# Earlier loads of the gate/up weights, and two corrected prices, in a planned transformer-block kernel

## The chip, the cores and the metric

The kernel runs on one core of a Trainium2 chip. That core has five engines with instruction queues of their own: TensorE (PE, matrix multiplications into the PSUM banks), VectorE (DVE), ScalarE (ACT), GpSimd (POOL) and SyncE (SP), which here only starts the transfers between memory and the on-chip buffer SBUF. The metric is device time in microseconds (us), the median of several runs. A measurement of this kernel can tell a change of about 0.2% (1.5 us) from none.

## The reference, cut to what matters

```python
xn = layernorm(x)                         # x: 2048 x 1024, bfloat16
q, k, v = split(xn @ wqkv)                # 32 heads of 32 columns
phi = lambda t: where(t > 0, t + 1, exp(t)) + 1e-6
pq, pk = phi(q), phi(k)
kv, z = einsum(pk, v), sum_over_rows(pk)  # per head
s = (pq @ kv) / (pq @ z + 1e-6) @ wo      # linear attention, 1024 columns
g = silu((silu(xn @ w_gate) * (xn @ w_up)) @ w_down)   # 3584 hidden columns
return x + s * g
```

## The kernel before, in words

All large products are computed with fast matrix multiplication of the Winograd-Strassen kind: seven half-size products take the place of eight, and the inputs and results of these are sums of blocks. For some of the seven products the scheme is applied a second time inside. So beside the matmuls there are many element-wise additions: of activations (`XF.outer`, `XF.inner`), of weights (`WF.combos` makes four sums of weight blocks, 1024 columns each; `WF.inner` makes up to eight smaller ones, of 256 and 512 columns) and of results (`Pair`).

The stages follow one another on TensorE: layer norm with the k and v projections (0 to about 120 us of the trace), the q projection (four "pairs", to about 195 us), gate and up (28 pairs over 14 groups of 256 columns, to about 520 us, with the softmax-free normalisation of q mixed in from the fourth pair to the eleventh), the attention output (four pairs, to about 575 us) and the down projection with the final gate (to the end). A pair is 1024 rows against 2 x 256 weight columns.

Nobody writes the order of the instructions by hand. Every operation is recorded in program order with what it reads and writes, and a planner (class `Plan`) then makes the order of each engine. It goes through all operations like a list scheduler with a price for each: at every step it takes the operation that can begin first, with ties broken by a due time `dl`. Each engine then runs its list strictly in order; semaphores hold it where a list item depends on another engine. The prices are only used to make the order. Three of the planner's rules matter here:

- **Weight loads.** `wload` records two transfers of 512 KB (gate and up, or the two halves of a q block), then `combos`. A load that is not marked `asap` gets, besides its true dependencies, a dependency on a TensorE step about 12 us ahead of its due time (`LEAD`, L316 and the loop over `o.sem` in `schedule`), so that it isn't started long before it is wanted. An `asap` load has none of that, and its due time is 6 us rather than 30 us behind the TensorE work recorded so far.
- **Where weights go.** There are three raw buffers (`raw_at`), three for the sums of four (`cmb_at`) and two for the inner sums (`inn_at`). Load number k takes raw buffer 0, 1, 0, 2, 1, 0, 2, ... The first two loads are the q blocks (Q0, Q1), then the groups G0 to G13 of gate and up, then four loads of normalised q for the attention output. Raw buffer 0 and raw buffer 2 are unused from the start; raw buffer 1 overlaps weights of the k and v stage.
- **The port.** VectorE and GpSimd share an SBUF port in the planner's view: an operation with `port = True` waits until GpSimd's current operation has ended, and GpSimd then waits for it. Marked are element-wise additions whose inputs both lie in SBUF, and line L1034.

GpSimd makes the inner sums of all gate/up weights (`IE`), and their sums of four except G0's (`CE`; G0's are VectorE's, `GC0`), 12 operations a group, and the inner sums of the attention output (`IS`). Everything else element-wise is on VectorE and ScalarE. All additions of `tt` are shown at line L478, all ScalarE operations at L470, all matmuls at L420.

`phi_evac` computes phi for a finished block: ScalarE's exponential, then L1034 (minimum and addition, fp16 in SBUF) and L1036 (maximum and addition), both on VectorE. L1036 reads the block from PSUM (`kind` "ps") or, where a last addition put the block into SBUF, from SBUF (`kind` "sb").

The names used below: "q pair (p, s)" is rows half p with q block s; "gate/up pair (p, n)" is rows half p with group n; x tiles are the 16 row tiles of the input; normalise operations are the additions' siblings at L478 that multiply phi(q) by 1/denominator.

Of the kernel before, what the change touches and what calls it, by code (L numbers as in the profile page):

```python
# [9 lines left out]
ALU = mybir.AluOpType  # L10
F32 = mybir.dt.float32
BF16 = mybir.dt.bfloat16
FP16 = mybir.dt.float16
KB = 1024
# [284 lines left out]
def build_kernel(nc, A_x, A_wqkv, A_wo, B_w_gate, B_w_up, B_w_down, out, WINDOW=20, NWARM=12, NIDLE=5, LEAD=12.0):  # L299
# [7 lines left out]
    NE = ("dve", "dve")  # L307
    CS, IS = ("dve",) * 4, ("pool",) * 8
    UBANK, PU = 0.0, 6.0
    N0, NA = 3, 2  # L310
    GC0 = ("dve",) * 4
    XE0 = XE1 = XE2 = XE3 = "dve"

# [8 lines left out]
    with ExitStack() as es:  # L322
# [61 lines left out]
        def tmp(pool):  # L384
            return VB(pool)

        def vap(v, dt=BF16, off=0, n=None):

            return SB.at(v.place + off, SIZE[v.pool.name] - off if n is None else n, dt)
# [4 lines left out]
        def sem(name):  # L394
            return es.enter_context(nc.semaphore(name))
# [4 lines left out]
        def dsem(name):  # L400
            if name not in semn:
                semn[name] = sem("d_" + name)
            return semn[name]
# [20 lines left out]
        def split(items):  # L424

            regs, vbs = [], []
            for x in items:
                if isinstance(x, VB):
                    regs.append(x.r)
                    vbs.append(x)  # L430
                else:
                    regs.append(x)
            return regs, vbs
# [22 lines left out]
        def op(eng, reads, writes, fn, busy, hold=(), **kw):  # L456
            rr, rv = split(reads)
            wr, wv = split(writes)

            mine = [v for v in rv if v.pool is BANK]  # L460
            wr += [v.r for v in mine if v not in wv]
            if mine:
                kw["urgent"] = kw.get("urgent", 0.0) + UBANK
            return PL.op(eng, rr, wr, fn, busy, vbs=rv + wv + list(hold), **kw)

        def ev(x):
            return x() if callable(x) else x

        def act(reads, writes, o, i, func, n, src="ps", **kw):
            return op("act", reads, writes, lambda h: h.activation(ev(o), ev(i), func, **kw),  # L470
                      n / 1200.0 + (0.055 if src == "ps" else 0.095) + (0.09 if "scale" in kw else 0.0)
                      + (0.09 if "bias" in kw else 0.0))

        def dve(reads, writes, fn, n, rate=0.96, **kw):
            return op("dve", reads, writes, fn, n / (rate * 1000.0) + 0.07, **kw)

        def tt(reads, writes, o, a, b, alu, n, fast=False, eng="dve"):
            f = lambda h: h.tensor_tensor(ev(o), ev(a), ev(b), alu)  # L478
            if eng == "pool":
                return op("pool", reads, writes, f, n / 610.0 + 0.42)  # L480
            q = dve(reads, writes, f, n, 1.92 if fast else 0.96)

            q.port = not any(isinstance(x, VB) and x.pool is BANK for x in reads)
            return q

        def dma(reads, writes, o, i, s, nbytes, tr=False, **kw):
            if tr:
                f = lambda h: h.dma_start_transpose(ev(o), ev(i))
            else:
                f = lambda h: h.dma_start(ev(o), ev(i))  # L490
            return op("sp", reads, writes, f, 1.25 if tr else 0.45, sem=s, nbytes=nbytes, **kw)
# [32 lines left out]
        class XF:  # L524
# [32 lines left out]
            def outer(self, parts):  # L557

                def g(nm):
                    return self.blk(nm) if parts == "all" else self.part(nm, parts)  # L560
                n = 2048 if parts == "all" else 512
                for o, a, b in (("T3", "R11", "R01"), ("T1", "R01", "R00"), ("T2", "R11", "T1"), ("T4", "R10", "T2")):
                    tt([g(a)[1], g(b)[1]], [g(o)[1]], g(o)[0], g(a)[0], g(b)[0], ALU.subtract, n, True)

            def inner(self, ms, eng="dve"):

                q = self.quad()
                bs = [JP.index(m) for m in ms]
                for u in range(0, len(bs), 2):
                    two = bs[u:u + 2]  # L570
                    lo, st = two[0], (two[1] - two[0] if len(two) > 1 else 1)

                    def cut(x):
                        return x[:, lo:two[-1] + 1:st]

                    def T(f):
                        o = self.j + f * 4 * KB
                        return cut(self.jform(f)[0]), both(*[SB.reg(o + b * KB, KB) for b in two])

                    def R(h, t):  # L580
                        return cut(q[:, :, h, :, t, :]), both(*[self.quarter_r(h, t, b) for b in two])
                    t2, t3, t4 = T(0), T(1), T(2)
                    for o, a, b in ((t3, R(1, 1), R(0, 1)), (R(0, 1), R(0, 1), R(0, 0)), (t2, R(1, 1), R(0, 1)),
                                    (t4, R(1, 0), t2)):
                        tt([a[1], b[1]], [o[1]], o[0], a[0], b[0], ALU.subtract, 512 * len(two), True, eng)
# [21 lines left out]
        class WF:  # L607
# [27 lines left out]
            def combos(self, eng):  # L635
                A = {(k, i): (self.v[:, :, 4 * k:4 * k + 4, i * 128:i * 128 + 128],
                              self.raw_r(None, range(4 * k, 4 * k + 4), i)) for k in range(2) for i in range(2)}
                C = [(self.c[:, q], self.cmb_r(q)) for q in range(4)]
                for n, (o, a, b, alu) in enumerate(((C[0], A[0, 1], A[1, 1], ALU.add), (C[1], C[0], A[0, 0], ALU.subtract),
                                                    (C[2], A[0, 0], A[0, 1], ALU.subtract),  # L640
                                                    (C[3], A[1, 0], C[1], ALU.subtract))):
                    tt([a[1], b[1]], [o[1]], o[0], a[0], b[0], alu, 1024, True, eng[n])
# [388 lines left out]
        def phi_evac(reads, src, kind, out_ap, out_r):  # L1031
            e = tmp(H1)
            act(reads, [e], partial(vap, e, FP16), src, ACT.Exp, 512, kind)
            dve([e], [e], lambda h: h.tensor_scalar(vap(e, FP16), vap(e, FP16), 1.0, EPS_PHI, ALU.min, ALU.add),  # L1034
                512, 3.84, urgent=PU).port = True
            dve(reads + [e], [out_r], lambda h: h.scalar_tensor_tensor(  # L1036
                out_ap, ev(src), 0.0, vap(e, FP16), ALU.max, ALU.add), 512, urgent=PU)

        kvb = [bank(leaves=False) for _ in range(3)]

# [189 lines left out]
        def wload(srcs, ceng, ieng, dt=BF16, reads=()):  # L1230
            k = wk[0]
            wk[0] += 1
            rk = (0, 1, 0)[k] if k < 3 else 2 - k % 3
            f = WF(raw_at[rk], cmb_at[k % 3], inn_at[k % 2], dt)
            for q, src in enumerate(srcs):
                if not isinstance(src, list):
                    src = [(slice(0, 8), src)]
                for kts, sr in src:
                    dma(list(reads), [f.raw_r(q, range(kts.start, kts.stop))], f.v[:, q, kts], sr,
                        dsem("wr%d_%d_%d" % (rk, q, kts.start)), 512 * KB // len(src))  # L1240
            f.combos(ceng)
            if ieng:
                f.inner(ieng, JQ)
            return f
# [3 lines left out]
        def q_load(s):  # L1248
            return wload([wqkv_v[:, :, (2 * s + q) * 256:(2 * s + q + 1) * 256] for q in range(2)], QC[s], QI[s])

        def gu_load(n):
            return wload([wg_v[:, :, n * 256:(n + 1) * 256], wu_v[:, :, n * 256:(n + 1) * 256]],
                         CE if n else GC0, None)
# [8 lines left out]
        def q_pair(p, s, wf, at=(), mix=()):  # L1262
            def evac(w, i, j, src, v, kind):
                g = 2 * (2 * s + w) + i
                o, orr = pq_tile(p, g, j)
                phi_evac([v], src, kind, o, orr)
            ST.pair(Pair(Prov(wf, XV[p]), evac, JQ), at, mix)
# [91 lines left out]
        def pq_load(p, j):  # L1359
            srcs = [[(slice(4 * k, 4 * k + 4), q_scr[p, k, j].rearrange("p (g t) -> p g t", t=512)[:, :, w * 256:(w + 1) * 256])  # L1360
                     for k in range(2)] for w in range(2)]
            return wload(srcs, CS, None, FP16, [named("q", p, k, j) for k in range(2)])
# [250 lines left out]
def bass_recurrent_scan__linear_attn_block__swiglu_ffn__prompt_kernel(  # L1613
    nc: bass.Bass,
    A_x: bass.AP,
    A_wqkv: bass.AP,
    A_wo: bass.AP,
    B_x: bass.AP,
    B_w_gate: bass.AP,
    B_w_up: bass.AP,  # L1620
    B_w_down: bass.AP,
    out: bass.AP,
):
    build_kernel(nc, A_x, A_wqkv, A_wo, B_w_gate, B_w_up, B_w_down, out)
# [28 lines left out]
```

## Time and profile before

| | |
|---|---|
| median of 16 runs | 761.14 us (756.64 to 763.69) |
| the profiled execution's own time | 760.1 us |
| its span, first to last instruction | 758.3 us |
| TensorE busy | 718.2 us (95%) |
| VectorE busy | 572.4 us (75%) |
| ScalarE busy | 358.7 us (47%) |
| GpSimd busy | 259.4 us (34%) |
| mean granted TensorE clock | 0.989 |

"Busy" counts the time in which an engine has an instruction in flight[...]. TensorE's busy time is all but the whole span, so what can be won without fewer matmuls is its idle time (about 40 us) and the time at a lowered clock.

By stage (TensorE busy, VectorE busy, GpSimd busy, of the stretch): 138 to 156 us: 17.73, 16.33 and 0.00 of 18; 164 to 195 us: 23.21, 29.59 and 23.82 of 31; 195 to 235 us: 37.40, 33.78 and 16.64 of 40; 235 to 335 us: 88.43, 87.51 and 64.76 of 100; 335 to 500 us: 165.00, 137.38 and 110.51 of 165.

### The profile page before, as it was taken

How to read it: one execution, taken by the hardware profiler on the slowest of the kernel's cores; microseconds unless marked ns; L12 is line 12 of the kernel's file. 1: busy time of each engine (PE TensorE's matmuls, PEld its weight loads, DVE VectorE, ACT ScalarE, POOL GpSimd, SP SyncE). 2: the span in 40 equal slices, each digit the busy share in tenths (PEclk: the TensorE clock that was granted, in tenths of full speed). 3: DMA queues.
4: the chain of work that ended last, by engine and by line, in shares of the span. 5: the costliest groups of instructions: out<-in, count | busy, mean ns of one | idle time of the engine just before them, and what ended most of it. 6: DMA issues, size and time to landing. Idle time of an engine off the chain costs nothing.

```text
span 758.3 us, 11444 instructions
## 1 busy us (share of the span) xinstructions
PE 718.2 (95%) x4091; PEld 388.5 (51%) x4121; DVE 572.4 (75%) x1107; ACT 358.7 (47%) x677; POOL 259.4 (34%) x230
## 2 busy tenths in 40 slices
PE   8999998896898988899999999999999999999996
PEld 4445454443455555556666666665554444444443
DVE  6999766989888789898888888879987662443433
ACT  3577554864546476564554554554565111111111
POOL 2111000029275478448765678802660000000000
PEclk9999999999999899999999999999999999999999
DMA  9343315250215536647333324145599382936421
GB/s 301 88 109 73 76 25 164 70 156 2 68 55 140 175 118 194 180 127 263 104 92 111 105 76 126 50 138 180 170 315 278 86 251 83 259 97 192 141 77 42
DMA packets 139801, 101.55 MB, mean 134 GB/s; under 512 B 18784, under 2 KB 132704, under 8 KB 139744
## 3 DMA queue, kind: packets, MB, share of 16 engines
q1 hardware_dynamic: 139744, 100.82, 44.6%
q8 instruction: 32, 0.52, 0.3%
q14 instruction: 25, 0.20, 0.1%
HBM read 68.16 MB, written 29.49 MB: 129 GB/s over the span
## 4 chain that ended last, share of the span: by engine, by line
PE 77%; DVE 16%; DMA 4%; issue 1%; ACT 1%; SPq 0%; ACTq 0%; DVEq 0%
PE ps L420 77%; DVE SB L478 8%; DVE ps L478 2%; DVE SB L1036 2%; DVE SB L1034 1%; DMA SB<-in_A_x_dram 1%; DMA SB<-h_scratch 1%; DMA SB<-in_B_w_up_dram 1%; ACT SB L470 1%; DMA SB<-m_scratch 1%; DVE stats L994 0%; DVE stats L995 0%; DVE SB L1286 0%; SPq L490 0%; DVE SB L1201 0%
## 5 line engine op out<-in xcount | busy, mean ns | idle before, releaser
L420 PE MATMUL ps<-SB 128*128 128x512 f16 (+3 forms) x3970 | 707.9, 338 | 31.3 <-DVE ps L478 10.6
L420 PEld LDWEIGHTS ps<-SB 128*128 128x128 f16 (+1 forms) x4000 | 382.6, 98 | 354.7 <-DVE ps L478 18.4
L478 POOL TENSOR_TENSOR SB<-SB 128x1024 f16<-128x1024 bf16 (+3 forms) x196 | 245.6, 1284 | 242.3 <-DMA SB<-in_B_w_up_dram 186.7
L470 ACT ACTIVATE SB<-ps 128x256 f32<-128x256 f32 (+4 forms) x397 | 214.4, 559 | 203.8 <-PE ps L420 190.7
L478 DVE TENSOR_TENSOR SB<-SB 128x512 f16<-128x512 f16 (+10 forms) x312 | 197.9, 667 | 71.7 <-DMA out_dram<-SB 21.6
L478 DVE TENSOR_TENSOR SB<-ps,SB 128x256 f32<-128x256 f32 (+2 forms) x318 | 182.7, 591 | 54.8 <-PE ps L420 49.9
L478 DVE TENSOR_TENSOR ps<-ps,SB 128x512 f32<-128x512 f32 (+1 forms) x238 | 122.3, 531 | 36.6 <-PE ps L420 31.4
L470 ACT ACTIVATE ps<-ps 128x512 f32<-128x512 f32 (+1 forms) x166 | 81.8, 494 | 120.8 <-PE ps L420 104.6
L470 ACT ACTIVATE SB<-SB 128x512 f16<-128x512 f32 x68 | 42.2, 620 | 57.8 <-DVE SB L478 57.2
L998 POOL TENSOR_TENSOR rstd<-veps,neg_half 128x1 f32<-128x1 f32 x16 | 11.2, 704 | 65.2 <-DVE veps L997 58.3
L1036 DVE SCALAR_TENSOR_TENSOR SB<-ps,SB 128x512 bf16<-128x512 f32 x49 | 32.9, 680 | 0.3
L1034 DVE TENSOR_SCALAR SB<-SB 128x512 f16<-128x512 f16 x64 | 23.3, 379 | 12.6 <-ACT SB L470 12.6
L470 ACT ACTIVATE SB<-SB,zc 128x512 bf16<-128x512 bf16 x32 | 22.1, 714 | 10.1 <-DVE SB L478 8.9
L470 ACT ACTIVATE SB<-SB,nmr,rstd 128x1024 f16<-128x1024 bf16 x12 | 14.8, 1234 | 1.1 <-DVE nmr L1000 1.0
L994 DVE BATCH_NORM_STATS2 stats<-SB 128x6 f32<-128x512 bf16 x16 | 11.0, 685 | 3.5 <-DMA SB<-in_A_x_dram 3.5
L1036 DVE SCALAR_TENSOR_TENSOR SB<-SB 128x512 bf16<-128x512 f32 x15 | 13.1, 876 | 0.1
L995 DVE BATCH_NORM_STATS2 stats<-SB 128x6 f32<-128x512 bf16 x16 | 10.9, 681 | 0.0
L420 PE MATMUL ps<-SB,ident 128*128 128x512 f16 x17 | 6.5, 558 | 1.4 <-POOL ident L501 1.4
L449 PE MATMUL ps<-ident,SB 128*128 128x128 f16 x40 | 3.0, 220 | 1.6 <-DVE SB L1201 1.0
L420 PEld LDWEIGHTS ps<-SB,ident 128*128 128x128 f16 x17 | 2.1, 131 | 4.5 <-issue 2.7
L1286 DVE RECIPROCAL SB<-SB 128x64 f32<-128x64 f32 x8 | 4.3, 539 | 0.0
L449 PEld LDWEIGHTS ps<-ident,SB 128*128 128x128 f16 x40 | 2.4, 98 | 3.5 <-DVE SB L1201 1.5
(28 smaller groups left out, 23.4 us busy)
## 6 DMA issues: line engine op xcount, KB each, us to landing
h_scratch<-SB SPq DMA_DIRECT2D x112, 128.0 KB, 1.7
SB<-h_scratch SPq DMA_DIRECT2D x16, 896.0 KB, 6.4
SB<-in_A_x_dram SPq DMA_DIRECT2D x32, 256.0 KB, 3.1
SB<-in_B_w_gate_dram SPq DMA_DIRECT2D x14, 512.0 KB, 4.1
SB<-in_B_w_up_dram SPq DMA_DIRECT2D x14, 512.0 KB, 5.3
SB<-in_B_w_down_dram SPq DMA_DIRECT2D x4, 1792.0 KB, 9.1
SB<-in_A_wqkv_dram SPq DMA_DIRECT2D x12, 512.0 KB, 6.8
SB<-r_scratch SPq DMA_DIRECT2D x32, 128.0 KB, 3.7
```

The lines of the kernel that those rows point to most:

```text
L420: last = h.matmul(o() if callable(o) else o, l() if callable(l) else l, r() if callable(r) else r, start=st, stop=sp, skip_group_check=True)
L449: last = h.transpose(o(), i(), ident[:, :])
L470: return op("act", reads, writes, lambda h: h.activation(ev(o), ev(i), func, **kw), n / 1200.0 + (0.055 if src == "ps" else 0.095) + (0.09 ...
L478: f = lambda h: h.tensor_tensor(ev(o), ev(a), ev(b), alu)
L994: dve([xr] + ([named("ve", 0)] if q == 1 else []), [sA], lambda h: h.bn_stats(stats[:, j, 0, :], xa[:, 0:512]), 512)
L995: dve([xr] + ([named("ve", 0)] if q == 1 else []), [sB], lambda h: h.bn_stats(stats[:, j, 1, :], xa[:, 512:1024]), 512)
L998: pool([ver, nh_r], [rsr], lambda h: h.tensor_tensor(rstd[:, j, :], veps[:, j, :], neg_half[:, :], ALU.pow), 0.56)
L1034: dve([e], [e], lambda h: h.tensor_scalar(vap(e, FP16), vap(e, FP16), 1.0, EPS_PHI, ALU.min, ALU.add), 512, 3.84, urgent=PU).port = True
L1036: dve(reads + [e], [out_r], lambda h: h.scalar_tensor_tensor(out_ap, ev(src), 0.0, vap(e, FP16), ALU.max, ALU.add), 512, urgent=PU)
L1286: dve([ea], [ra], lambda h, q=q: h.reciprocal(vap(ra, F32)[:, q * 64:q * 64 + 64], vap(ea, F32)[:, q * 64:q * 64 + 64]), 400)
```

## The change

Three edits, none of which changes what is computed or on which engine:

```diff
-    N0, NA = 3, 2
+    N0, NA, WA = 3, 2, True
...
             if eng == "pool":
-                return op("pool", reads, writes, f, n / 610.0 + 0.42)
+                return op("pool", reads, writes, f, n / 531.0 + 0.2)
...
             dve(reads + [e], [out_r], lambda h: h.scalar_tensor_tensor(
-                out_ap, ev(src), 0.0, vap(e, FP16), ALU.max, ALU.add), 512, urgent=PU)
+                out_ap, ev(src), 0.0, vap(e, FP16), ALU.max, ALU.add), 512, urgent=PU).port = kind == "sb"
...
                     dma(list(reads), [f.raw_r(q, range(kts.start, kts.stop))], f.v[:, q, kts], sr,
-                        dsem("wr%d_%d_%d" % (rk, q, kts.start)), 512 * KB // len(src))
+                        dsem("wr%d_%d_%d" % (rk, q, kts.start)), 512 * KB // len(src), asap=WA)
```

The first and the last make all of `wload`'s transfers `asap`: the q blocks, gate and up, and the loads for the attention output. The second changes the planner's price of a GpSimd addition: 2.10 to 2.13 us for 1024 columns, 1.26 to 1.16 us for 512, 0.84 to 0.68 us for 256. The third makes L1036 a port operation where it reads from SBUF.

Since the planner makes the order anew, every engine's list changes. The set of instructions is the same. The larger moves:

- SP's list. The two loads of Q0 and the two of G1, which stood after the last transposes and after the m_scratch stores, stand behind the transfers of x tiles 0 to 5 and of the k and v weights: Q0's two and G1's gate ahead of x tiles 6 and 7, G1's up ahead of x tiles 8 and 9. Each later gate and up load stands a few stores earlier, and the two are apart, each with its own wait on TensorE.
- GpSimd's list. G1's four sums of 1024 columns come before G0's inner sums instead of after them, and G1's inner sums are mixed with G0's. After that each group's four sums mostly stand together ahead of its inner sums.
- VectorE's and ScalarE's lists are reordered throughout, by a few places mostly; TensorE's list as well, within the planner's window of 20 steps.

## The prediction

> **What bounds the kernel now.** First the page's sums: TensorE is busy 718.2 of 758.3 us, so I looked for its gaps. The table of 20 us stretches puts them at the start, at 120 to 140 us and between 160 and 340 us; from 340 to 500 us TensorE has none, and nothing on another engine can be won there. TensorE's own timeline, reduced to rows with idle time in front (in brackets: us, and who ended it), has three large gaps:
>
> ```profile
> 181.20 4.46 PE L420 MATMUL ps<-SB 128*128 128x256 f16 x20 [4.82 <-DVE SB L1036]
> ...
> 247.60 32.30 PE L420 MATMUL ps<-SB 128*128 128x256 f16 x192 [3.62 <-DVE SB L478]
> ...
> 323.61 193.44 PE L420 MATMUL ps<-SB 128*128 128x256 f16 x1232 [3.31 <-DVE ps L478]
> ```
>
> All end on VectorE. The chain of waits names the work ahead of the first:
>
> ```profile
> 174.06 3.96 DVE SB L1034 x4
> 178.02 3.13 DVE SB L1036 x2
> ```
>
> Four L1034 take 3.96 us, whose median is 284 ns; 0.60 of the 3.13 us is an L1036 from PSUM, so the one from SBUF takes 2.5. The groups by shape show it for all:
>
> ```profile
> L1036 DVE SCALAR_TENSOR_TENSOR SB<-ps,SB 128x512 bf16<-128x512 f32 x49 | 32.9, 680 | 0.3
> L1034 DVE TENSOR_SCALAR SB<-SB 128x512 f16<-128x512 f16 x64 | 23.3, 379 | 12.6 <-ACT SB L470 12.6
> L1036 DVE SCALAR_TENSOR_TENSOR SB<-SB 128x512 bf16<-128x512 f32 x15 | 13.1, 876 | 0.1
> L478 POOL TENSOR_TENSOR SB<-SB 128x1024 f16<-128x1024 bf16 x39 | 84.6, 2184 | 105.6 <-DMA SB<-in_B_w_up_dram 105.4
> ```
>
> A stretched VectorE operation is about as long as a GpSimd sum of 1024 columns (2184 ns). The timeline at the second gap agrees, VectorE and then GpSimd:
>
> ```profile
> 240.40 5.48 DVE L478 TENSOR_TENSOR SB<-SB 128x512 f16<-128x512 bf16 x3
> 238.06 10.09 POOL L478 TENSOR_TENSOR SB<-SB 128x1024 f16<-128x1024 bf16 x7
> ```
>
> Last, busy time and granted clock (the 1.00 or less behind GpSimd's count) behind each gap:
>
> ```profile
> 181.00:185.00 4.00, 3.80 (x16) 2.17 (x17) 2.59 (x6) 1.95 (x4) 4.00 (x3) 0.57 0.00 0
> 246.00:253.00 7.00, 5.40 (x18) 2.64 (x19) 4.08 (x8) 1.57 (x4) 6.15 (x7) 0.51 0.17 56
> 324.00:328.00 4.00, 4.00 (x21) 2.35 (x19) 4.00 (x6) 3.19 (x7) 3.92 (x5) 0.58 0.13 49
> ```
>
> After each gap TensorE runs at half clock: that loses another 3.80 x 0.43 = 1.6, 5.40 x 0.49 = 2.7 and 4.00 x 0.42 = 1.7 us. So the three cost 6.4, 6.3 and 5.0 us, 5.9 on average: a third of all that can be won.
>
> [...] L1036 from SBUF stretches (to 2.6 us), L1036 from PSUM never does (at most 692 ns). [...] gaps of 3.3 to 4.8 us lead to half clock, the next largest after 20 us (1.93) doesn't. [...] Here x tiles issued at 3.83 us land 8.4 us later behind the weights.
>
> **The change, part by part.** Sums are against the profiled execution, 760.1 us (span 758.3); the runs' median is 1.04 higher.
>
> *Loads at the start.* Q0 and G1 move up, Q0 from 91 us and G1 from 165 us. Q0's pieces and G1's gate, 1.5 MB, lie ahead of x tiles 6 and 7 in SP's queue. [...] 1.5 MB at the measured 303 GB/s delay them by 5 us, from landing near 20 us (6 MB at that rate) to near 25; VectorE first reads them at 32.4. The up load (0.5 MB, 1.7 us) meets tiles 8 and 9 (issued 23.2, read at 38.8) and the first transposes (26.7, landing in 3.1, read at 32.1), which keep under 1 us. If that cover fails, VectorE, full from 12 to 37 us, stops: +2. I take +0.2. Q0's sums can't move: their buffers hold k and v data till about 120.
>
> *G1's sums.* Now GpSimd runs them at 175.5 to 184.6 us, across the first gap. Their buffer is last read by TensorE, one quarter after another, at 138, 146, 149 and 152 us by the trace's semaphore records, and the new list puts them there. GpSimd is empty then, and G0's inner sums behind them wait for weights until 161.2, so they delay nothing on GpSimd. What is left of GpSimd after 161 ends some 9 us earlier. Gains: the five stretched operations at 174 to 180 us take 6.5 us, unstretched 1.8; of the 4.7 between, 4.3 lie behind 175.5, on these sums. Short inner sums (0.7 to 1.2 us) take their place at about half a length for each of four, 1.8, so the gap shrinks by 2.5. It is then under 3.3, so the half clock goes: 1.6. Of the stretched ones at 186 to 190 (2.4 us) TensorE, idle 2.0 us at 185 to 193, gets 1.2. Cost: seven port operations lie at 149 to 155 us; two sums hold each up to 1.9 us, 3.8 together, against VectorE's 1.7 us of idle in the 18 from 138. TensorE is full there and has results in hand: I take 1.3. Sum: -4.0. If all waits moved rather than went: +1; if the whole first event goes free: -7.6.
>
> *G2 to G7.* The semaphore records give when the buffer is free: 184/190, 220/221, 242/243, 271/273, 298/299 and 327/329 us (gate/up), where the loads were issued at 200, 227, 256, 280, 308 and 336. So GpSimd begins each group 6 to 16 us earlier. Its work isn't awaited by TensorE (no such row in the waits), so this is worth nothing by itself; what counts is where the sums of 1024 fall. G3's, landing 5.7 us after 221, end near 235.5, so the three operations at 240.4 meet short inner sums: their 5.48 us become about 3.3, the gap 1.4: -2.2, and -2.7 for the clock. G6's end near 313.5, so the gap at 320.3 shrinks by 1.4 and loses its half clock: -3.1. Against this, G5's would begin near 278, just where six normalise operations lie (277 to 283), and in the new list two of them stand ahead of G4's last sum and two right behind G3's. I count one new event of the average size, +5.9. Sum: -2.1.
>
> *G8 on.* 7 to 8 us earlier, TensorE full: 0. *Attention output.* Its first load comes 14 to 31 us earlier, out of the way of the m_scratch loads; TensorE idles 1.8 us at 500 to 545: -0.6 (-1.5 to +1).
>
> *SP's queue.* Gate and up wait for TensorE separately, with h stores queued behind them. Freeing comes 1.3 to 1.5 us apart (for G2 6), so a store waits about that long; h buffers are twelve. 0; a store chain that emptied them would stop ScalarE.
>
> *L1036's mark* affects 15 operations, with (876 - 680) x 15 = 2.9 us of waiting in all, part of the sums above. *GpSimd's prices*: new 2.13/1.16/0.68, measured 2.18/1.21/0.74 to 0.86, so the group of twelve is priced 15.9 rather than 16.8, its measured length 15.5 to 17.0: no clear correction. Only through the order: 0, within the range.
>
> Sum: 0.2 - 4.0 - 2.1 - 0.6 = -6.5, so 753.6 for this execution, 754.6 for the median.
>
> **Rivals.** Let n be the number of new events, a pair of port operations under sums of 1024; each is 5.9 and the rest of the sum is -12.4. For an event speaks that 40 additions with both inputs in SBUF lie at 160 to 335 us and that the planner's times are not the chip's; against it that the planner now starts loads from buffers TensorE frees, and knows L1036's wait.
> - None: 748.7. Needs the new order to fit the chip's times everywhere.
> - Two: 760.5, no change. GpSimd's work has only been moved against VectorE's.
> - Slower: three or more, in the normalise stage, where GpSimd is busy 65% and VectorE 88%. 5.3 x 1 over, so 766.4 for three. It decides from n = 2.1 on. The before has three events in all; the new order would need as many among the groups G2 to G7 and G1's new place.
> - The early loads don't help since their transfers are paced by the buffers anyway: true from 340 us on, and it would leave the first gap, about 760.
>
> **How the numbers follow.** Likeliest, n = 1: 0.38, own range 751 to 758. None: 0.15. Two, or mere moving: 0.21, of which 0.09 faster, 0.08 same, 0.04 slower, since about 0.2% (1.5 us) is what can be told from none. Three or more: 0.26, of which 0.02 same. Faster 0.38 + 0.15 + 0.09 = 0.62, same 0.10, slower 0.28. The range leaves out half of n = 0 and those beyond three: 748 to 766.
>
> **What would show it.** Right: GpSimd's 1024 sums at 138 to 154 us; the 4.82 us gap under 3 and no half clock near 181; GpSimd's wait for up weights (186.7 us) much smaller; L1036 from SBUF at a mean near 700 ns. Wrong: new half-clock stretches between 195 and 335 us, normalise operations over 1 us behind sums of 1024, or VectorE waiting for x tiles before 40 us.

## The result, and the profile after

The changed kernel takes 748.24 us (median of 9 runs, 746.22 to 750.75), the kernel before 760.94 beside it (median of 48 runs). The ratio is 0.983, with a 95% interval of 0.9811 to 0.9849: faster by 12.7 us, about twice the 6.5 us that the prediction summed up. The profiled execution took 747.62 us, its span is 745.9, TensorE is busy 713.7 us of it and the mean clock is 0.995. Of the 12.4 us by which the span shrank, 4.5 are TensorE's busy time (between 130 and 560 us it runs at half clock for 3.4 us, in the kernel before for 13.7) and 7.9 its idle time.

TensorE's timeline between 130 and 340 us, changed kernel, rows with over 1.5 us of idle time in front (start, length, what ran, in brackets the idle time and who ended it):

```profile
136.18 0.81 PE L420 MATMUL ps<-SB 128*128 128x256 f16 x4 [1.58 <-ACT ps L470]
...
176.89 8.44 PE L420 MATMUL ps<-SB 128*128 128x512 f16 x46 [1.72 <-DVE SB L478]
...
258.57 27.95 PE L420 MATMUL ps<-SB 128*128 128x256 f16 x174 [2.37 <-DVE SB L478]
```

The three gaps of 4.82, 3.62 and 3.31 us are gone, and so is the one of 1.93 us at 281.8. The chain of waits ahead of 177 us still has the same four L1034:

```profile
172.98 3.25 DVE SB L1034 x4
176.24 0.60 DVE SB L478
177.17 1.19 DVE SB L1036 x2
```

The groups by shape (busy us, mean ns; then idle before) and the wait of GpSimd for the up weights (us in all, times, longest) are:

```profile
L1036 DVE SCALAR_TENSOR_TENSOR SB<-ps,SB 128x512 bf16<-128x512 f32 x49 | 32.4, 678 | 0.1
L1034 DVE TENSOR_SCALAR SB<-SB 128x512 f16<-128x512 f16 x64 | 23.8, 388 | 12.1 <-ACT SB L470 12.1
L1036 DVE SCALAR_TENSOR_TENSOR SB<-SB 128x512 bf16<-128x512 f32 x15 | 12.5, 843 | 0.0
```

```profile
POOL SB L478 <- DMA SB<-in_B_w_up_dram: 89.0, 13, 8.1
```

GpSimd waits for up weights 89.0 us rather than 186.7, so the loads do come early. But the operations that GpSimd's sums hold are hardly shorter: L1036 from SBUF 843 ns against 876, L1034 388 against 379. To see all of VectorE's waiting at once, I took from each trace, for every kind and shape of VectorE operation, the time by which an instance exceeds the lower quartile of its kind: 43.5 us before, 44.4 after. The waiting has not gone. It lies elsewhere: of the operations held for over 1 us between 195 and 335 us there were six before (begun at 217, 240, 243, 291, 318 and 321 us) and two after (253 and 255).

Where the time went shows in the busy times by stretch. Columns: stretch, its length; busy time (and instructions) of TensorE's matmuls, its weight loads, VectorE, ScalarE, GpSimd; granted clock; share and GB/s of the transfers. The kernel before:

```profile
0.00:138.00 138.00, 129.30 (x714) 63.07 (x728) 112.40 (x275) 81.32 (x136) 13.86 (x34) 1.00 0.42 116
138.00:164.00 26.00, 25.27 (x167) 13.55 (x168) 22.49 (x56) 19.93 (x42) 1.17 (x1) 1.00 0.39 118
164.00:195.00 31.00, 23.21 (x115) 10.96 (x114) 29.59 (x48) 16.28 (x30) 23.82 (x19) 0.94 0.14 36
195.00:235.00 40.00, 37.40 (x262) 22.17 (x261) 33.78 (x68) 18.89 (x40) 16.64 (x12) 1.00 0.38 107
235.00:335.00 100.00, 88.43 (x535) 53.17 (x534) 87.51 (x153) 61.14 (x118) 64.76 (x48) 0.95 0.47 143
335.00:500.00 165.00, 165.00 (x1066) 103.70 (x1064) 137.38 (x248) 84.90 (x174) 110.51 (x84) 1.00 0.38 116
500.00:570.00 70.00, 68.09 (x412) 39.39 (x411) 62.77 (x104) 38.17 (x79) 28.66 (x32) 1.00 0.71 221
```

The changed kernel:

```profile
0.00:138.00 138.00, 127.06 (x701) 61.22 (x714) 109.78 (x270) 79.75 (x132) 14.11 (x34) 1.00 0.46 123
138.00:164.00 26.00, 22.68 (x116) 11.30 (x116) 25.37 (x51) 19.54 (x39) 8.82 (x4) 0.93 0.29 91
164.00:195.00 31.00, 28.20 (x181) 14.34 (x180) 29.87 (x57) 18.43 (x36) 15.31 (x16) 1.00 0.20 59
195.00:235.00 40.00, 38.50 (x273) 23.52 (x272) 36.57 (x73) 21.49 (x44) 28.51 (x20) 1.00 0.27 82
235.00:335.00 100.00, 94.55 (x601) 57.52 (x599) 91.41 (x168) 64.11 (x126) 65.36 (x49) 1.00 0.56 180
335.00:500.00 165.00, 163.77 (x1048) 101.78 (x1047) 136.31 (x247) 83.21 (x170) 101.27 (x79) 1.00 0.35 110
500.00:570.00 70.00, 69.91 (x413) 39.99 (x412) 61.26 (x101) 41.91 (x84) 28.74 (x31) 1.00 0.77 237
```

With the idle time as stretch less busy time, and the loss at a low clock estimated as stretch times what is missing to 1.00, the change comes to:

| stretch, us | idle | clock | sum |
|---|---|---|---|
| 0 to 138 | +2.2 | 0 | +2.2 |
| 138 to 164 | +2.6 | +1.8 | +4.4 |
| 164 to 195 | -5.0 | -1.9 | -6.9 |
| 195 to 335 | -7.2 | -5.0 | -12.2 |
| 335 to 500 | +1.2 | 0 | +1.2 |
| 500 to 570 | -1.8 | 0 | -1.8 |

The sum is -13.1, 0.7 more than the span shows, since the stretches hold slightly different work. Nearly all of the gain lies in the stage where normalisation and gate/up overlap, 195 to 335 us.

### The profile page after: what moved, and what is told of

The parts are those of the page before. It is cut to its first block, busy times and chain, and to the rows that moved or that the text cites. A ratio compares the mean times of both kernels' runs of the same rounds, so it can differ in the third digit from the quotient of the medians.

```text
span 745.9 us, 11430 instructions
## 1 busy us (share of the span) xinstructions
PE 713.7 (96%) x4092; PEld 386.4 (52%) x4121; DVE 568.5 (76%) x1107; ACT 358.4 (48%) x677; POOL 262.1 (35%) x230
## 4 chain that ended last, share of the span: by engine, by line
PE 75%; DVE 18%; issue 2%; DMA 2%; ACT 2%; SPq 0%; ACTq 0%; DVEq 0%
PE ps L420 75%; DVE SB L478 9%; DVE SB L1036 3%; DVE ps L478 2%; DVE SB L1034 2%; ACT SB L470 1%; DMA SB<-in_A_x_dram 1%; DMA SB<-SB 1%; DVE stats L994 1%; DVE stats L995 1%; ACT ps L470 0%; DVE SB L1286 0%; DVE Zh L1205 0%; SPq L490 0%; DVE SB L1201 0%
## 5 line engine op out<-in xcount | busy, mean ns | idle before, releaser
L470 ACT ACTIVATE SB<-SB 128x512 f16<-128x512 f32 (+1 forms) x68 | 42.2, 621 | 77.5 <-DVE SB L478 74.7
L1034 DVE TENSOR_SCALAR SB<-SB 128x512 f16<-128x512 f16 x64 | 23.8, 388 | 12.1 <-ACT SB L470 12.1
L1036 DVE SCALAR_TENSOR_TENSOR SB<-ps,SB 128x512 bf16<-128x512 f32 x49 | 32.4, 678 | 0.1
L1036 DVE SCALAR_TENSOR_TENSOR SB<-SB 128x512 bf16<-128x512 f32 x15 | 12.5, 843 | 0.0
```

The source lines that it names most:

```text
L1036: dve(reads + [e], [out_r], lambda h: h.scalar_tensor_tensor(out_ap, ev(src), 0.0, vap(e, FP16), ALU.max, ALU.add), 512, urgent=PU).port = ...
```

## The experiments

Four theories were set against each other, and the expectations name them so. A: early loads let GpSimd's long sums (1024 columns) run clear of VectorE's port operations. B: better prices give a better order. C: any new order is a draw, and that of before was a poor one. D: it is the order of VectorE's work and the times of GpSimd's sums that must fit each other, so early loads without the new order, or the new order without early loads, gain nothing. "Held" says that a VectorE operation takes longer than it does without a GpSimd sum beside it: the trace shows it as one long instruction, an L1036 from SBUF of 2.60 us beside long sums and of 0.79 with these cut. "The port" is the planner's name for what holds it; which part of the chip that is, no run shows. All ratios are against the kernel before on the same chip, with 95% intervals.

### The edits one by one

The loads alone (first and last edit of the diff), the mark on L1036 alone, the new price alone, and then the loads with one of the other two. Mark and price together without the loads were not tried.

```diff
# loads alone
+    N0, NA, WA = 3, 2, True
+                        dsem(...), 512 * KB // len(src), asap=WA)
# mark alone
+                out_ap, ev(src), 0.0, vap(e, FP16), ALU.max, ALU.add), 512, urgent=PU).port = kind == "sb"
# price alone
+                return op("pool", reads, writes, f, n / 531.0 + 0.2)
```

> The earlier loads alone, without the two price corrections. Theory A (the loads move GpSimd's sums of 1024 columns away from VectorE's port operations, and that is the gain): most of the 1.7%, 748 to 752 us, no half-clock stretch between 160 and 335 us. Theory B (the gain is the better order that the planner makes once it knows L1036's wait and GpSimd's times): 758 to 762 us. Theory C (any new order lands somewhere between 748 and 766 by chance, and the parts don't add up): anything, and the sum of the parts alone is not the whole.

> The port mark of L1036 from SBUF alone. Theory A: 759 to 762 us, since only 2.9 us of waiting in all is at stake. Theory B: 752 to 757 us. Theory C: anything within 748 to 766.

> GpSimd's new price alone. Theory A: 759 to 763 us, no change, since the new price of a group of twelve is no nearer to the measured one than the old. Theory B: 752 to 758 us. Theory C: anything within 748 to 766.

> Earlier loads and the port mark, with GpSimd's old price. Theory A: 747 to 751 us, the whole gain. Theory B: about 752 to 757, as the port mark alone. Theory C: not the sum of the two parts alone.

> Early loads and the new price of GpSimd's additions, without the mark on L1036; it completes the set of one, two and three edits. If the edits' effects add (loads -1.14%, price -0.74%), ratio 0.981, as the whole change, and the mark is worth nothing. If the mark is what makes the loads fit (loads with mark gave 0.987, loads alone 0.989), about 0.988 and half clocks after 200 us. If each order is a matter of chance, anything between 0.980 and 1.0.

| kernel | median us | ratio | 95% interval |
|---|---|---|---|
| loads | 752.04 | 0.9886 | 0.9829 to 0.9943 |
| mark | 761.40 | 1.0018 | 1.0001 to 1.0035 |
| price | 754.50 | 0.9926 | 0.9905 to 0.9947 |
| loads + mark | 750.33 | 0.9868 | 0.9812 to 0.9924 |
| loads + price | 753.91 | 0.9901 | 0.9880 to 0.9921 |
| all three | 748.24 | 0.9830 | 0.9811 to 0.9849 |

The effects don't add: the price is worth 0.7% alone, where theory B had it, and on top of the loads it costs 0.15%. Nor do the loads alone do what theory A asked: the time is at the edge of its range, but half clock comes in at 183 and 204 us (granted clock 0.97 from 138 to 195 us, 0.91 from 195 to 235). What holds is the mean: the four kernels with early loads have a mean ratio of 0.987, the three without (the kernel before among them) 0.998. The mark's three comparisons give +0.2, -0.2 and -0.7%, the price's -0.7, +0.2 and -0.4%. So the loads carry about 1.1%; the other two can't be told from the scatter of orders, which the last experiment measures.

### Is it the port?

If the port is what it is about, the gain must vanish once GpSimd's sums are short. In two kernels each weight sum on GpSimd is cut to the first 8 columns of its last dimension, a sixteenth of its columns in all, in the kernel before and in the changed one; in a third only the sums of 1024 columns, in the kernel before. The rest of these sums is left out of the computation. The order of all lists and the prices stay as they were.

```diff
-                return op("pool", reads, writes, f, n / 610.0 + 0.42)
+                return op("pool", reads, writes, lambda h: h.tensor_tensor(cut(ev(o)), cut(ev(a)), cut(ev(b)), alu), n / 610.0 + 0.42)
...
+def cut(x):
+    return x[(slice(None),) * (len(x.shape) - 1) + (slice(0, 8),)]
```

> The kernel before with each of GpSimd's weight sums cut to 8 columns of its last dimension (the rest of the sums is left out), the order unchanged: GpSimd holds the port for a small part of the time. What it gains is the whole price of the port waits. Theory A and D: three gaps, three half clocks and the smaller waits go, 738 to 746 us. If the port is not the cause: 757 to 762 us.

> The changed kernel with GpSimd's weight sums cut in the same way (the rest left out). Theory A and D: what the change gained was port waits, so with these gone in both the two short kernels lie within 4 us of each other: 738 to 746 us. If the gain came from the order apart from the port: it is kept, some 10 us below the short kernel before.

> The kernel before with its order unchanged; only GpSimd's additions of 1024 columns are cut to 8 columns, so that part of the sums of four weight blocks is left out; the inner sums are whole. With all of GpSimd's weight sums cut the time was 734.6, 26.6 us less. The prediction let only the long sums cost anything: about 735 to 738 by it. If the cost goes by GpSimd's busy time (52 long sums at 2.18 us are 113 of 259 us), 26.6 x 0.44 = 12, so about 749.

The kernel before with short sums takes 734.62 us (ratio 0.9657, 0.9618 to 0.9695), the changed one 731.93 (0.9629, 0.9593 to 0.9665), both below the forecast, and with only the long sums cut the kernel before takes 741.80 (0.9747, 0.9725 to 0.9770). So GpSimd's sums cost the kernel before 26.6 us and the changed one 748.24 - 731.93 = 16.3. With sums this short (the waiting counted as above is 6.0 and 5.7 us), the two orders are 2.7 us apart instead of 12.7: some 10 us of the gain come from where GpSimd's sums fall. That TensorE waited for the sums themselves is ruled out: in the traces of both kernels there is no such wait. The long sums alone cost 761.56 - 741.80 = 19.8 us, three quarters of it, though they are 112.4 of the 250.6 us of these sums. The small ones are not free: about 7.

VectorE's timeline shows this at one place. The third kernel has the list of before, so the operations are the same. First the kernel before, then the one with its long sums cut:

```profile
173.99 4.04 DVE L1034 TENSOR_SCALAR SB<-SB 128x512 f16<-128x512 f16 x4
177.95 2.60 DVE L1036 SCALAR_TENSOR_TENSOR SB<-SB 128x512 bf16<-128x512 f32 x1
```

```profile
175.23 2.23 DVE L1034 TENSOR_SCALAR SB<-SB 128x512 f16<-128x512 f16 x4
177.38 0.79 DVE L1036 SCALAR_TENSOR_TENSOR SB<-SB 128x512 bf16<-128x512 f32 x1
```

The same five operations take 6.6 us beside the long sums and 3.0 beside small and cut ones; TensorE's gap there falls from 4.82 to 1.50 us. Left out work also ends earlier, so the 26.6 and 19.8 us are upper bounds on what the held operations cost.

### Early loads without the new order, and the new order without early loads

One kernel keeps every compute list of before and only moves the weight loads in SP's list to right behind what frees their buffer. The other has all lists of the changed kernel, but the loads of G2 to G13 get back the TensorE step that held them. Both helpers act after planning and touch SP's list alone: `early` takes the `LEAD` step from each weight load and moves the load up, `held` gives it back and moves the load down.

```diff
# lists of before, loads early (on the kernel before)
-                        dsem(...), 512 * KB // len(src))
+                        dsem(...), 512 * KB // len(src)).wl = True
-        prog = PL.emit(esem)
+        early(PL); prog = PL.emit(esem)
# lists of the change, loads late (on the changed kernel)
-        prog = PL.emit(esem)
+        held(PL); prog = PL.emit(esem)
```

> The lists of TensorE, VectorE, ScalarE and GpSimd are those of the kernel before, word for word, and their buffers too; only the weight transfers start as soon as their buffer is free (Q0's and G1's behind the first fourteen transfers). GpSimd then begins G2 to G13 some 6 to 14 us earlier, while G1's sums stay behind G0's inner sums. Theory A in its plain form (earlier sums by themselves miss VectorE's port operations at 240 and 320 us): those two gaps and their half clocks go, 8 us, and new collisions near 280 us give some back: 751 to 757 us. Theory D (the new order of VectorE's list is what misses the sums, and the earlier loads only let the planner make it): 759 to 766 us, collisions elsewhere.

> The lists of the changed kernel, but the loads of G2 to G13 are held back by the TensorE step of the old rule, so that GpSimd begins each group 6 to 14 us later than the order was made for. Theory A: the collisions come back, 755 to 762 us. Theory D: they come back as well, perhaps more (756 to 766), since the order fits the early sums. If neither the sums' place nor the port matters: 748 to 750 us.

Early loads with the old order: 777.32 us, ratio 1.0216 (1.0181 to 1.0252), 16 us slower than before. The new order with late loads: 765.44, 1.0063 (1.0044 to 1.0083), 17 us slower than the changed kernel and 5 slower than before. TensorE's timeline of the first (rows of over 3.5 us of idle time):

```profile
181.40 4.46 PE L420 MATMUL ps<-SB 128*128 128x256 f16 x20 [5.13 <-DVE SB L1036]
...
203.02 0.61 PE L420 MATMUL ps<-SB 128*128 128x256 f16 x2 [3.87 <-DVE SB L478]
...
263.99 7.76 PE L420 MATMUL ps<-SB 128*128 128x512 f16 x38 [5.20 <-DVE ps L478]
...
297.67 15.01 PE L420 MATMUL ps<-SB 128*128 128x512 f16 x86 [8.39 <-DVE ps L478]
```

And what lies ahead of the largest, on VectorE and on GpSimd in the same kernel:

```profile
286.62 10.38 DVE L478 TENSOR_TENSOR SB<-SB 128x512 f16<-128x512 bf16 x7
```

```profile
287.28 9.44 POOL L478 TENSOR_TENSOR SB<-SB 128x1024 f16<-128x1024 bf16 x4 [6.89 <-DMA SB<-in_B_w_up_dram]
```

Four of these seven operations take 2.33 us each, a long sum's length, where the kernel before took 0.41. There they were over at 281.2 us and this group's sums began at 286.1; with early loads the sums begin while the operations run. The other three gaps have such holds ahead of them as well. This refutes A as it stood: earlier loads by themselves move the long sums onto port operations as readily as off them, and the loss is 11 us beyond what D forecast. With the old order, early loads don't gain.

The kernel with the new order and late loads doesn't show the other half of D. Its largest gap, 5.35 us, ends at 238.48, with four long sums running from 233.40. But the chain of waits ahead of it leads elsewhere:

```profile
228.89 5.73 DMA SB<-r_scratch
...
236.02 2.42 DVE SB L478 x2
```

The first row is a load of the denominators for the normalisation. In SP's list it stands right behind the weight loads that are held back: it is issued at 228.89 us and lands 5.73 us later, where the changed kernel issues it at 225.17 and has it 2.84 us later. One of the two normalise operations behind it is held, 2.07 us for 0.41. The gaps that end at 267.05 and 297.63 go back to such loads too, and ScalarE waits 13.3 us for them between 195 and 335 us, in the changed kernel not at all. So this kernel loses at least in part by SP's queue, and what the new order is worth without early loads stays open.

One number of the first kernel matters for the prediction: at the end of the k and v stage (131 us) it is only 0.1 us behind the kernel before, measured at the same TensorE step, although Q0's and G1's loads stand between the x tiles (G1's gate is issued at 17.2 us, its up at 20.0). Their transfers cost all but nothing.

### Q0 and G1 late

```diff
-                        dsem(...), 512 * KB // len(src), asap=WA)
+                        dsem(...), 512 * KB // len(src), asap=WA and k not in (0, 3))
```

> The changed kernel, but the loads of Q0 and of G1 are not marked: they stand where the kernel before had them, and G1's sums follow G0's inner sums again. The loads of Q1, G0 and G2 onwards are early. The prediction's terms for these two loads were +0.2 at the start and -4.0 for G1's sums: by them this kernel is 3.8 us slower than the changed one, about 752. By the progress measured since (start +2.3 us, q projection about -2.2 us net) the two cancel: 748, with the first gap and its half clock back near 181 us and the start 1 to 2 us quicker. If the order after 200 us is a matter of chance, since every list is planned anew, it is anything from 748 to 760, with half clocks between 235 and 335 us.

757.79 us, ratio 0.9945 (0.9931 to 0.9959): by the ratios 8.8 us slower than the changed kernel, neither 3.8 nor 0. It has no half clock after 213 us (1.00 from 235 to 335), so chance did not strike where it was expected. The start is not quicker for it (1.9 us behind the kernel before at 131 us, where the changed one is 2.3 behind). At the TensorE step that the kernel before reaches at 206 us it is 7.8 us behind, the changed one 0.1: the first event is back, with a second behind it.

```profile
183.81 7.17 PE L420 MATMUL ps<-SB 128*128 128x256 f16 x30 [3.83 <-DVE SB L1036]
203.55 0.61 PE L420 MATMUL ps<-SB 128*128 128x256 f16 x4 [2.08 <-DVE ps L478]
```

```profile
180.55 2.60 DVE L1036 SCALAR_TENSOR_TENSOR SB<-SB 128x512 bf16<-128x512 f32 x1
```

So the early places of Q0 and G1 together are worth more than the -3.8 of the prediction in this pair of orders, near the best case of -7.6 for G1. It is one draw of an order, though, and the next two experiments tell how much such a draw may vary.

### A better price for the landing

```diff
-                        dsem(...), 512 * KB // len(src), asap=WA)
+                        dsem(...), 512 * KB // len(src), asap=WA).pad = 1.5
```

> The changed kernel; the planner is also told that a weight load lands 1.5 us later than it had assumed (it assumed about 4.0 us from issue to landing, the trace shows 5.3 to 5.7). If what counts is that the planned order fits the times at which GpSimd's sums really run, this fits better and some of the 16.3 us that the port still costs go: 742 to 746. If the fit has been good enough, or an order is good or bad by chance, 746 to 758, slower as likely as not.

749.84 us, 0.9843 (0.9809 to 0.9878): not to be told from the changed kernel. VectorE's waiting, counted as above, falls from 44.4 to 36.5 us, and 6 operations instead of 16 are held by over 0.3 us beside a long sum. But two gaps of 4.19 and 3.44 us, at 180 and 200 us, come in, with half clock behind both (the run's mean clock is 0.993). Less waiting did not mean less time.

### How much is chance?

To measure what a new order does by itself, three prices that have nothing to do with the change were shifted a little, in the kernel before and in the changed one: 0.02 us on a VectorE addition, 0.03 us on a ScalarE operation, 0.8 ns on a matmul. Compared place by place, the shifts change 30 to 46% of VectorE's list, where the change itself has 42%; of GpSimd's list they change less, 12 to 26% for its 51%.

```diff
# VectorE
-            return op("dve", reads, writes, fn, n / (rate * 1000.0) + 0.07, **kw)
+            return op("dve", reads, writes, fn, n / (rate * 1000.0) + 0.09, **kw)
# ScalarE
-                      n / 1200.0 + (0.055 if src == "ps" else 0.095) + (0.09 if "scale" in kw else 0.0)
+                      0.03 + n / 1200.0 + (0.055 if src == "ps" else 0.095) + (0.09 if "scale" in kw else 0.0)
# TensorE
-                         len(mms) * max(n / 2400.0 + 0.0012, 0.03) if cost is None else cost, vbs=rv + [b],
+                         len(mms) * max(n / 2400.0 + 0.0020, 0.03) if cost is None else cost, vbs=rv + [b],
```

> The kernel before, planned anew with a VectorE addition priced 0.02 us higher, so that about as many lists differ as in the change under study; loads, mark and GpSimd's prices are those of before. If every order is a draw by chance and that of before was a poor one, this lands between 748 and 756, near the changed kernel with the same shift. If early loads with the new prices do the work, it stays at 757 to 765, 8 to 14 us above its partner.

> The changed kernel with the same 0.02 us on a VectorE addition. By chance alone: anything from 748 to 762, no better than its partner on average. If the change does the work: 745 to 752, 8 to 14 us below its partner.

> The kernel before, planned anew with a ScalarE operation priced 0.03 us higher. By chance alone: 748 to 762. If the change does the work: 757 to 765, 8 to 14 us above its partner.

> The changed kernel, planned anew with a ScalarE operation priced 0.03 us higher. By chance alone: 748 to 762. If the change does the work: 745 to 752, 8 to 14 us below its partner.

> The kernel before, planned anew with each matmul priced 0.8 ns higher. By chance alone: 748 to 762. If the change does the work: 757 to 765, 8 to 14 us above its partner.

> The changed kernel, planned anew with each matmul priced 0.8 ns higher. By chance alone: 748 to 762. If the change does the work: 745 to 752, 8 to 14 us below its partner.

| shift | before: us, ratio (interval) | changed: us, ratio (interval) |
|---|---|---|
| none | 760.94, 1 | 748.24, 0.9830 (0.9811 to 0.9849) |
| VectorE | 759.71, 0.9995 (0.9976 to 1.0015) | 745.74, 0.9800 (0.9760 to 0.9841) |
| ScalarE | 758.88, 0.9963 (0.9944 to 0.9982) | 756.42, 0.9938 (0.9920 to 0.9956) |
| TensorE | 762.89, 1.0032 (1.0015 to 1.0049) | 751.26, 0.9888 (0.9845 to 0.9932) |

The mean ratio is 0.9998 in the left column (standard deviation 0.28%) and 0.9864 in the right one (0.61%). The distance is 1.34%, or 10.2 us, with a standard error of 0.34% from the four orders of each. So the kernel before was not a poor draw, theory C doesn't explain the gain, and the change is worth about 10 us on the mean of these orders. With four of each, that is known to some 3 to 17 us only (an estimate at 95% from the standard error). A single order of the changed kernel lies 5 us to one side or the other: the three shifted pairs are 14.0, 2.5 and 11.6 us apart, and the second of them falls well short of the 8 to 14 forecast. The order of the change under study is 2 to 3 us better than the mean of its kind, and the first shift gives one that is better still, 745.74 us, by the same chance. (The changed kernel with ScalarE's shift left no trace that can be compared.) VectorE's waiting, by the count above, is 43.5, 44.9, 47.1 and 48.8 us in the left column and 44.4, 37.4 and 40.0 in the three traces of the right one: 5.5 us less on average, where the kernel gains 10.

## Why the prediction was right and wrong

**Right: the direction and what bounds the kernel.** TensorE starves behind VectorE operations that are stretched beside GpSimd's long sums (in the kernel before 4.82 us of idle time behind an L1036 of 2.60 us), and the clock adds to it (0.50 from 181.30 to 184.71 us). Cutting the sums showed 26.6 us of cost, and with the sums cut the changed kernel is only 2.7 us ahead. The time that came is that of the rival without any new event, 748.7, but that is chance: a new event did come, and other terms made up for it.

**The start: +0.2, measured +2.2.** The loads of Q0 and G1 cost nothing, as the step said: with them moved alone the kernel was 0.1 us behind at 131 us, and VectorE's waits for x tiles are 3.4 us after, 3.5 before. Newly planned lists are 0.0 to 2.8 us behind there, whether these loads are early or not; the list of before with short sums is 1.3 behind, so part of it is chance. What it is in the new lists was not settled.

**G1's sums: -4.0, measured -2.5.** This is 4.4 - 6.9 of the table. The sums were expected at 138 to 154 us; GpSimd's timeline has them at 142 to 160:

```profile
142.03 2.13 POOL L478 TENSOR_TENSOR SB<-SB 128x1024 f16<-128x1024 bf16 x1 [62.93 <-PE ps L420]
149.93 2.12 POOL L478 TENSOR_TENSOR SB<-SB 128x1024 f16<-128x1024 f16 x1 [5.78 <-PE ps L420]
154.84 2.13 POOL L478 TENSOR_TENSOR SB<-SB 128x1024 f16<-128x1024 bf16 x1 [2.79 <-PE ps L420]
157.66 2.44 POOL L478 TENSOR_TENSOR SB<-SB 128x1024 f16<-128x1024 bf16 x1 [0.69 <-PE ps L420]
```

The first gap shrank from 4.82 to 1.72 us (expected under 3) without half clock (1.00 from 164 to 195 us), and the gain there was 6.9 us for the 5.3 of the prediction's three terms. What came out otherwise is the cost, put at 1.3 us. On VectorE

```profile
150.36 1.84 DVE L1034 TENSOR_SCALAR SB<-SB 128x512 f16<-128x512 f16 x1
...
157.45 3.21 DVE L1036 SCALAR_TENSOR_TENSOR SB<-SB 128x512 bf16<-128x512 f32 x2
```

are three operations, of which the first and the last are held, 5.1 us where 1.6 would do: one under the second sum, one under the fourth, which ran past 154. "TensorE is full there and has results in hand" was too sure: it idles 3.3 us of the 26 from 138, 2.6 more than before. By the chain of waits 1.1 us of this, the gap that ends at 153.72, come from the first of the two; the largest gap, 1.35 us at 161.74, ends on ScalarE with no held operation ahead of it. So the sums' own cost is shown for 1.1 us and not for the rest. The other 1.8 us are a half-clock stretch, 0.50 from 138.01 to 141.42 us. It follows idle time that lies ahead of any sum of G1, so it is not their doing; without it the term is -4.3, near the forecast.

**G2 to G7: -2.1, measured -12.2.** This is the step that failed. Its terms were -8.0 for the second and third gap and +5.9 for one new event. The new event came on G4's sums, one of the places that the prediction named, but small. VectorE, then GpSimd:

```profile
252.55 4.43 DVE L478 TENSOR_TENSOR SB<-SB 128x512 f16<-128x512 bf16 x2
```

```profile
248.15 10.11 POOL L478 TENSOR_TENSOR SB<-SB 128x1024 f16<-128x1024 bf16 x6 [6.03 <-DMA SB<-in_B_w_up_dram]
```

Two normalise operations take 4.43 us. They cost one gap, 2.37 us, and no clock (1.00 from 235 to 335 us): 2.4 for the 5.9 that I had counted from the mean of three events. And the two old gaps did not shrink to 1.4 and 1.9 us, they went, and the one of 1.93 us at 281.8 with them: 8.9 us of idle time for the 3.6 that I had counted. The clock's share of the old gaps was nearly right (-4.4 expected, -5.0 measured). I had moved GpSimd's sums under an otherwise unchanged VectorE order, and that kernel was made: early loads with the old lists lose 16 us. The planner had moved both. Which of its moves took the two gaps away was not tried one by one.

**G8 on: 0, measured +1.2.** TensorE now idles 1.2 us of 165. **Attention output: -0.6, measured -1.8,** outside its range of -1.5 to +1 by 0.3: TensorE's idle time at 500 to 570 us is gone. Measured at the same TensorE steps, from 498 to 560 us, all newly planned kernels with early loads for the attention output gain 1.8 to 3.1 us on the kernel before, those with late ones 1.0 at most, so this part is not a draw.

**L1036's mark and GpSimd's prices: 0 each.** The expectation that L1036 from SBUF would come near 700 ns was wrong: 843. That the mark by itself does nothing was right (1.0018). The price alone gave 0.7%, which is no more than two or three standard deviations of a mere shift.

**What was not foreseen: how far an order can be a draw.** The range 748 to 766 was wide enough for this, but the text gave its width to events to be counted, and the same change with ScalarE's price shifted gave 756.42.

## What to carry to other kernels

When a planner makes the order, don't price an early load by moving its consumer over the old timetable: both timetables change, and here the early loads under the old order lost 16 us, where with an order planned for them they won 12.7. When loads are moved in SP's list, look at what stands behind them: with the held loads it was a small transfer behind them that came late, issued at 228.89 us instead of 225.17 and landed 5.73 us later instead of 2.84. Judge such a change by three or four orders of each kind (shift an unrelated price), for one order may be off by 5 us. And look at what a wait starves, not at the sum of the waits: that of VectorE was all but the same in the two kernels.

## What the runs showed of the hardware

**Half clock came in stretches of 3.41 us, and similar idle time did or did not bring it.** I had read the half clock as following a gap of 3.3 us or more. In the kernel before the granted clock is 0.50 from 181.30 to 184.71 us, from 246.16 to 252.98 and from 324.67 to 328.08, in the changed kernel from 138.01 to 141.42: by the traces' record of the clock 3.413 us each time, or twice that (6.827). In the kernel before the second and third begin 64.86 and 143.37 us behind the first, 19.0 and 42.0 times 3.413 us. So these stretches fit a grid of 3.413 us, and each trace can be laid on the grid of its own half clock (columns as above; TensorE's busy time is the first, the clock is behind GpSimd's count), first the kernel before:

```profile
177.88:181.30 3.42, 0.10 (x1) 0.10 (x2) 3.42 (x4) 0.00 (x0) 3.42 (x2) 1.00 0.00 0
...
321.26:324.67 3.41, 1.06 (x10) 0.96 (x11) 3.41 (x6) 1.82 (x4) 3.41 (x4) 1.00 0.07 18
324.67:328.08 3.41, 3.41 (x14) 1.83 (x13) 3.41 (x5) 2.65 (x6) 3.33 (x4) 0.50 0.15 60
```

and the changed kernel, two stretches of its grid and one that straddles them:

```profile
254.04:257.46 3.42, 2.16 (x12) 0.98 (x10) 3.42 (x3) 2.08 (x5) 3.34 (x3) 1.00 0.00 0
257.46:260.87 3.41, 2.30 (x17) 1.68 (x18) 3.38 (x8) 0.00 (x0) 1.46 (x3) 1.00 0.61 231
255.20:258.61 3.41, 1.04 (x7) 0.32 (x5) 3.41 (x5) 1.24 (x3) 2.98 (x3) 1.00 0.23 94
```

The straddling one is as idle as that at 321.26 (TensorE busy 1.04 and 1.06 us), but its halves lie in two stretches that are each over 60% busy (2.16 and 2.30 of 3.41 us), and the clock stays at 1.00. From 11 us on, six stretches of the two grids were busy 36% or less (0.10 to 1.24 us), and each was followed by half clock; all others at full clock were busy 55% or more, and none of them was. Once at half clock it stayed there behind the one stretch that was 58% busy (1.97 us, from 246.16) and left it behind the four that were busy throughout. Where between 36 and 55% it changes, these two traces don't show.

The two kernels hold a test of this that nobody planned. Around 134 us both run the same matmuls with the same gaps, of 1.58 and 0.72 us, the changed kernel 2.3 us later. In the kernel before the gaps fall into two stretches of its grid, in the changed kernel into one:

```profile
130.10:133.51 3.41, 2.22 (x19) 1.35 (x16) 3.41 (x10) 2.66 (x5) 0.00 (x0) 1.00 0.00 0
133.51:136.92 3.41, 2.20 (x14) 1.06 (x14) 3.41 (x11) 1.88 (x5) 0.00 (x0) 1.00 0.11 38
```

```profile
134.60:138.01 3.41, 1.09 (x7) 0.51 (x8) 3.41 (x13) 2.53 (x6) 0.00 (x0) 1.00 0.11 38
```

The kernel before stays at full clock (1.00), the changed one has half clock (0.50) from 138.01 us. So a gap of 1.58 us with other idle time beside it cost half clock, and one of 2.37 us at 258 did not: the first is bad luck and the second good luck, of some 1.7 us each (an estimate, half of 3.41 us).

**VectorE operations were held beside short GpSimd sums too.** The inner sums, 0.7 to 1.2 us each, cost the kernel before some 7 of 26.6 us, by the difference of the two kernels with cut sums. Its trace has both sizes side by side: an L1034 takes 2.20 us beside a sum of 1024 columns of 2.16 us, and the one ahead of it 0.75 beside a sum of 256 columns of 0.72, where the median is 0.28. Each of the two ends 0.14 to 0.15 us after its sum.
